# A three-stage kernel on one Trainium2 core: the last two chunks' second layers by eight plain products, added up in the PSUM banks, with totals and shares scaled ahead

## The chip, the cores and the metric

The kernel runs on one core of a Trainium2 chip. The metric is the device time of one execution in microseconds (us). Engine names as in the profile: PE is TensorE's matmuls, PEld its weight loads, DVE is VectorE, ACT is ScalarE, POOL is GpSimd, SP is SyncE, which here only issues transfers.

## The reference, cut to what matters

```python
x  = retention(q, k, v)                    # (2304, 512)
g  = np.maximum(x @ w_in, 0.0) ** 2        # first block, d_ff 2048
x  = g @ w_out                             # (2304, 512)
p  = probs / (probs.sum(-1, keepdims=True) + 1e-9)
for e in range(4):                         # four experts, 1024 hidden each
    h    = np.maximum(x @ w1[e], 0.0)
    out += p[:, e:e+1] * (h @ w2[e])
```

Everything is fp32; each product of two fp32 matrices is done as three matmuls, high part by high part, high by low and low by high.

## The kernel before, in words

Tokens are cut into five groups: four of 512 and one of 256. The hidden dimension is cut into chunks of 256: 8 chunks for the first block (numbers 0 to 7) and 16 for the experts. The experts' chunks are gone through twice. Pass 1 (chunks 8 to 23) serves groups 0, 1 and 4, and keeps the split weights in DRAM (`keep`). Pass 2 (chunks 24 to 39) serves groups 2 and 3 together, fetches the kept weights (`fetch`), and is where the change lies. `NW` is 40, so `NW - 2` and `NW - 1` are chunks 38 and 39; `split_w2`, for chunks 22 and 23, makes the second-layer weights of both.

In pass 2 both layers are done by a seven-product scheme (Strassen and Winograd) over 2 by 2 blocks. The first layer of a chunk (`first_layer`) is seven products of six matmuls each: A11 and then A12 into bank b1, S2 into b6, S3 and then A22 into b7, S1 and then S4 into b5. ACT copies the half-done b1 into `u0` (L865), before A12 is added into that bank; DVE adds (`add`, L853) and does relu times the token's expert share in one instruction (`relu`, L856). The shares lie in `rows` (`prow[3]` is the last expert's). Each result becomes an operand (`operand`, which calls `split`): ACT casts the high part (L130), POOL subtracts for the low part (L131). POOL also makes the differences t1 to t4 that the second layer needs (`minus`, L859); their operands are put off into the following chunk by the list `later`.

The second layer of chunk c (`second_layer`) runs one chunk later, in seven steps between the products of chunk c + 1's first layer: R4, H12, R3, H11, R1, R2, H22. A step is two banks with three matmuls each. R3 goes into the banks that hold R4, and H11 into those that hold H12, so that R3 waits until DVE has added R4 alone into its total, and H11 likewise. DVE adds every step into the totals e1 to e4 (`gather`, L939, two instructions a step). So a chunk is 42 + 42 matmuls.

The last chunk's second layer (`outputs`) is eight products of six matmuls each without the scheme, each with a bank of its own (a "place"): the totals are settled first (e2 gets e1 on DVE at L1129; POOL makes e3 and e4 at L992); then each place is added to its total (L1010), multiplied by the token's scale `back` (L1014 on DVE, L1012 on POOL) and sent out (L1017). `back` comes from DRAM and is halved on ACT (L987). The last place is done in two halves of 256 columns.

Every engine takes its instructions in the order in which the code issues them; a wait holds up all that stand behind it on that engine. The PSUM pool gives the 8 banks out in turn.

Of the kernel before, what the change touches and what calls it, by code (L numbers as in the profile page):

```python
# [6 lines left out]
F32 = mybir.dt.float32  # L7
# [4 lines left out]
ALU = mybir.AluOpType  # L12
# [14 lines left out]
NW1, NW2 = 8, 16  # L27
# [6 lines left out]
def tile_kernel(ctx, tc, qkT, kvn, v4d, mask, kdec, wd, w, probs, probs2, out, outT):  # L34
# [138 lines left out]
    def split_w2(c):  # L173

        hi = wp.tile([128, 2 * W2C], F32R, name="w2hi")
        lo = wp.tile([128, 2 * W2C], F32R, name="w2lo")
        w2t[c] = hi, lo
        w2s[c] = [t[:, :W2C].rearrange("p (f n) -> p f n", f=FT) for t in (hi, lo)]
        blk = [slice(BC * i, BC * (i + 1)) for i in range(8)]
        if c < NW1:  # L180
            for i in range(4):
                r = wraw.pop((c, 4 + i))
                yield from from_f64(r, hi[:, blk[i]], lo[:, blk[i]])
                load_piece()
# [361 lines left out]
    with tc.manual_schedule():  # L546
# [259 lines left out]
                    nc.sync.dma_start(out=out[tt * 128 : (tt + 1) * 128, :], in_=acc)  # L806

        spare = []
        taken, ops, prow, sums, later, loads = [0], {}, [], [], [], []

        def operand(src):
            t = gp.tile([128, FT, GT], F32R, name="ghi" if taken[0] % 2 else "glo")
# [15 lines left out]
        def first_layer(c):  # L828
# [33 lines left out]
            t3 = wrp.tile([128, GT], F32, name="wraw")  # L862
            b1 = bank()
            product(b1, A11, 7)
            nc.scalar.copy(out=u0, in_=b1)  # L865
# [29 lines left out]
            add(b11, b5, u1)  # L895
            relu(b11, b11, 1)
            o["11"] = operand(b11)

            def one():
                o["t1"] = operand(b12)  # L900
# [8 lines left out]
            def four():  # L909
                o["t4"] = operand(b21)  # L910

            if c < NW - 1:
                minus(b12, b12, b11)
                later.extend((one, two, three, four))
            yield
# [62 lines left out]
        def outputs(c):  # L978

            w2h, w2l = w2t[c]  # L980
            o = ops.pop(c)
            v = nc.vector
            back = []
            for i in range(2):
                t = wrp.tile([128, GT], F32, name="wraw")
                nc.sync.dma_start(out=t, in_=units_[i : i + 1, :].rearrange("o n -> (o n)").partition_broadcast(128))
                nc.scalar.activation(out=t, in_=t, func=ACTF.Copy, scale=0.5)  # L987
                back.append(t)
            e1, e2, e3, e4 = totals()
            for a, b in ((e3, e2), (e4, e3)):  # L990
                for d in range(2):
                    nc.gpsimd.tensor_tensor(out=a[d], in0=b[d], in1=a[d], op=ALU.subtract)  # L992
            for e, half, g, xs in (
                (e2, 0, 0, ("12", "22")), (e1, 0, 1, ("11", "21")), (e3, 1, 0, ("12", "22")), (e4, 1, 1, ("11", "21"))
            ):
                for d in range(2):
                    b = ps.tile([128, GT], F32, name="h", tag="ps")
                    n = 0
                    for f in range(2):
                        i = (H11, H12)[f] + half  # L1000
                        for a, y in ((w2h, 0), (w2h, 1), (w2l, 0)):
                            nc.tensor.matmul(
                                b, a[:, BC * i + 128 * d : BC * i + 128 * d + 128], o[xs[f]][:, y, :],
                                start=(n == 0), stop=(n == 5),
                            )
                            n += 1
                    r, m = 256 * half + 128 * d, GT // 2 if (half, g, d) == (1, 1, 1) else GT
                    for j in range(0, GT, m):
                        p = slice(j, j + m)
                        v.tensor_tensor(out=e[d][:, p], in0=e[d][:, p], in1=b[:, p], op=ALU.add)  # L1010
                        if (half, g, d) in ((0, 1, 0), (0, 1, 1), (1, 0, 0)):
                            nc.gpsimd.tensor_tensor(out=e[d], in0=e[d], in1=back[g], op=ALU.mult)  # L1012
                        else:
                            v.scalar_tensor_tensor(  # L1014
                                out=e[d][:, p], in0=e[d][:, p], scalar=1.0, in1=back[g][:, p], op0=ALU.mult, op1=ALU.mult
                            )
                        nc.sync.dma_start(out=outT[r : r + 128, GT * g + j : GT * g + j + m], in_=e[d][:, p])  # L1017

        def layer2(job):
            c, gs = job  # L1020
# [93 lines left out]
                s = scale(g, rest[:1])  # L1114
        sums += [yp.tile([128, 4, GT], F32, name=f"sums{i}", tag=f"acc{i}") for i in (2, 3)]
        for c in range(NW1 + NW2 + 1, NW):
            f, t = first_layer(c), second_layer(c - 1)
# [5 lines left out]
            if c == NW - 1:  # L1123
                for i in range(4):
                    next(t)
                    if i == 2:
                        e1, e2, _, _ = totals()
                        for d in range(2):
                            nc.vector.scalar_tensor_tensor(  # L1129
                                out=e2[d], in0=e1[d], scalar=1.0, in1=e2[d], op0=ALU.mult, op1=ALU.add  # L1130
                            )
# [3 lines left out]
        outputs(NW - 1)  # L1135


def _host(inputs):
# [75 lines left out]
```

## Time and profile before

| | us |
|---|---|
| time, median of 3 runs (lowest to highest) | 1205.81 (1205.4 to 1208.23) |
| time of the profiled execution | 1205.93 |
| its span, first to last instruction | 1204.1 |
| PE busy | 1188.4 (99% of the span) |
| DVE busy | 905.5 (75%) |
| POOL busy | 687.1 (57%) |
| ACT busy | 425.6 (35%) |

The profiled execution took 1.83 us more than its span. Start times in rows count from the first instruction. A matmul's row shows 0.39 us although one starts every 0.227 us, since they are pipelined; gaps between starts are the thing to read.

### The profile page before, as it was taken

How to read it: one execution, taken by the hardware profiler on the slowest of the kernel's cores; microseconds unless marked ns; L12 is line 12 of the kernel's file. 1: busy time of each engine (PE TensorE's matmuls, PEld its weight loads, DVE VectorE, ACT ScalarE, POOL GpSimd, SP SyncE). 2: the span in 40 equal slices, each digit the busy share in tenths (PEclk: the TensorE clock that was granted, in tenths of full speed). 3: DMA queues.
4: the chain of work that ended last, by engine and by line, in shares of the span. 5: the costliest groups of instructions: out<-in, count | busy, mean ns of one | idle time of the engine just before them, and what ended most of it. 6: DMA issues, size and time to landing. Idle time of an engine off the chain costs nothing.

```text
span 1204.1 us, 18090 instructions
## 1 busy us (share of the span) xinstructions
PE 1188.4 (99%) x6448; PEld 1001.1 (83%) x6448; DVE 905.5 (75%) x1543; ACT 425.6 (35%) x976; POOL 687.1 (57%) x686
## 2 busy tenths in 40 slices
PE   7999999999999999999999999999999999999997
PEld 7888888888888888888888888888888888888886
DVE  5877677787787689477877778777867787878778
ACT  3445433333333346534234334333412222222221
POOL 4656545455555426566444544644327777777777
PEclk9999999999999999999999999999999999999999
DMA  9921111111111100645355435555497546464551
GB/s 331 313 88 53 44 45 53 45 45 44 44 53 45 36 1 19 236 167 227 139 211 202 158 121 194 206 215 209 154 320 277 200 168 237 143 233 156 211 175 70
DMA packets 66513, 177.18 MB, mean 147 GB/s; under 512 B 9204, under 2 KB 17652, under 8 KB 66424
## 3 DMA queue, kind: packets, MB, share of 16 engines
q1 hardware_dynamic: 66136, 175.82, 41.0%
q8 instruction: 51, 0.84, 0.3%
q14 instruction: 38, 0.31, 0.1%
q10 hardware_dynamic: 288, 0.21, 0.1%
HBM read 113.33 MB, written 62.68 MB: 146 GB/s over the span
## 4 chain that ended last, share of the span: by engine, by line
PE 93%; DVE 4%; POOL 1%; ACT 1%; issue 1%; DMA 0%; SPq 0%; DVEq 0%; ACTq 0%
PE h L597 20%; PE o L793 17%; PE o L762 16%; PE h L631 13%; PE h L846 12%; PE h L929 11%; PE xo L438 1%; PE xo L450 1%; DVE pt L399 1%; PE qk L385 1%; DVE xl L721 1%; PE state L416 0%; DMA kv_n<-kvn 0%; DVE xl L473 0%; DVE sums L1010 0%
## 5 line engine op out<-in xcount | busy, mean ns | idle before, releaser
L131 POOL TENSOR_TENSOR glo<-r,ghi 128x512 fp32r<-128x512 f32 (+1 forms) x78 | 95.1, 1219 | 150.7 <-ACT ghi L130 136.6
L597 PE MATMUL h<-xl,w1hi 128*128 128x512 f32 (+1 forms) x448 | 154.0, 344 | 0.0
L597 PE MATMUL h<-xh,w1hi 128*128 128x512 f32 (+1 forms) x448 | 154.0, 344 | 0.0
L597 PE MATMUL h<-xh,w1lo 128*128 128x512 f32 (+1 forms) x448 | 153.9, 344 | 0.0
L801 DVE SCALAR_TENSOR_TENSOR oacc<-o,pr,oacc 128x512 f32<-128x512 f32 x150 | 109.6, 744 | 27.6 <-PE o L793 27.3
L939 DVE TENSOR_TENSOR sums<-sums,h 128x512 f32<-128x512 f32 x202 | 128.3, 677 | 1.2 <-PE h L929 1.2
L793 PE MATMUL o<-w2hi,ghi 128*128 128x512 f32 x320 | 124.8, 390 | 0.1
L793 PE MATMUL o<-w2hi,glo 128*128 128x512 f32 x320 | 124.7, 390 | 0.0
L793 PE MATMUL o<-w2lo,ghi 128*128 128x512 f32 x320 | 124.5, 389 | 0.0
L762 PE MATMUL o<-glo,w2hi 128*128 128x512 f32 (+1 forms) x320 | 117.8, 368 | 0.0
L762 PE MATMUL o<-ghi,w2hi 128*128 128x512 f32 (+1 forms) x320 | 117.7, 368 | 0.0
L762 PE MATMUL o<-ghi,w2lo 128*128 128x512 f32 (+1 forms) x320 | 117.7, 368 | 0.0
L605 DVE TENSOR_TENSOR r<-r 128x512 f32<-128x512 f32 (+1 forms) x72 | 58.0, 806 | 58.1 <-ACT r L601 57.9
L597 PEld LDWEIGHTS h<-xh,w1hi 128*128 128x128 f32 x448 | 84.8, 189 | 10.8
L597 PEld LDWEIGHTS h<-xl,w1hi 128*128 128x128 f32 x448 | 84.9, 189 | 10.6
L597 PEld LDWEIGHTS h<-xh,w1lo 128*128 128x128 f32 x448 | 84.8, 189 | 10.0
L770 DVE TENSOR_TENSOR y<-o,y 128x512 f32<-128x512 f32 (+1 forms) x140 | 86.1, 627 | 3.5 <-PE o L762 3.4
L846 PE MATMUL h<-xh,w1hi 128*128 128x512 f32 x224 | 88.1, 394 | 0.2 <-ACT r L865 0.2
L631 PE MATMUL h<-xh,w1lo 128*128 128x512 f32 x224 | 87.3, 390 | 0.0
L846 PE MATMUL h<-xh,w1lo 128*128 128x512 f32 x224 | 87.3, 390 | 0.0
L631 PE MATMUL h<-xh,w1hi 128*128 128x512 f32 x224 | 87.2, 389 | 0.0
L846 PE MATMUL h<-xl,w1hi 128*128 128x512 f32 x224 | 87.2, 389 | 0.0
(167 smaller groups left out, 2867.4 us busy)
## 6 DMA issues: line engine op xcount, KB each, us to landing
wraw<-wd SPq DMA_DIRECT2D x64, 256.0 KB, 2.7
wraw<-w SPq DMA_DIRECT2D x64, 256.0 KB, 2.9
kept<-w2hi SPq DMA_DIRECT2D x15, 768.0 KB, 4.3
kept<-w2lo SPq DMA_DIRECT2D x15, 768.0 KB, 6.0
w2hi<-kept SPq DMA_DIRECT2D x14, 768.0 KB, 5.1
w2lo<-kept SPq DMA_DIRECT2D x14, 768.0 KB, 6.7
qkt<-qkT SPq DMA_DIRECT2D x16, 576.0 KB, 6.1
kv_n<-kvn SPq DMA_DIRECT2D x16, 512.0 KB, 5.6
```

Of the source, the lines that this page charges most:

```text
L131: engine.tensor_tensor(out=lo, in0=src, in1=f32(hi), op=ALU.subtract)
L385: nc.tensor.matmul(qk[:, j, w : w + m], k_t[p, o : o + C], q_t[p, o : o + m], start=True, stop=True, skip_group_check=True,)
L597: nc.tensor.matmul(h, wk(a, f, k), group(x, g, k), start=(n == 0), stop=(n == 3 * KT - 1))
L605: nc.vector.tensor_tensor(out=r, in0=r, in1=r, op=ALU.mult)
L631: nc.tensor.matmul(o, a[:, i, k, :], slot(x, j)[:, k, :], start=(first and n == 0), stop=(n == 5), skip_group_check=True,)
L762: nc.tensor.matmul(o, a[:, f, 128 * m : 128 * m + 128], x[:, f, :], start=(n == 0), stop=(n == 3 * FT - 1))
L770: nc.vector.tensor_tensor(out=y, in0=o, in1=y, op=ALU.add)
L793: nc.tensor.matmul(o, a[:, f, 128 * m : 128 * m + 128], x[:, f, :], start=(n == 0), stop=(n == 3 * FT - 1))
L801: nc.vector.scalar_tensor_tensor(out=acc, in0=o, scalar=pr[:, tt, e : e + 1], in1=acc, op0=ALU.mult, op1=ALU.add)
L846: nc.tensor.matmul(o, a[:, i, k, :], slot(x, j)[:, k, :], start=(first and n == 0), stop=(n == 5), skip_group_check=True,)
L929: nc.tensor.matmul(b, a[:, BC * i + 128 * d : BC * i + 128 * d + 128], o[x][:, y, :], start=(first and n == 0), stop=(n == 2), skip_group_ ...
L939: v.tensor_tensor(out=e, in0=e, in1=b, op=op)
```

## The change

Chunks 38 and 39 no longer make t1 to t4 and t3. Both second layers are done by eight plain products (`plain_second`): chunk 38's go into eight banks (four new ones, and the four of chunk 39's first layer as they come free), and chunk 39's are added on top in the same banks, so that DVE adds one result to each total instead of gathering chunk 38's seven steps. The totals are settled and multiplied by `back` during chunk 39's first layer (`settle`), and the last expert's shares are multiplied by `back` before chunk 38 (`scale_shares`), so that its and chunk 39's results come out scaled already. `back` is loaded at the start of chunk 37 (`load_back`). For chunk 22 the four derived weight blocks are not made, kept or fetched.

```diff
-        whole = c < NW1 + NW2 - 1
+        whole = c < NW1 + NW2 - 2
...
-        return ((0, 1), (2, 8)) if c % NW2 != NW1 - 1 else ((0, 4),)
+        return ((0, 1), (2, 8)) if c % NW2 not in (NW1 - 2, NW1 - 1) else ((0, 4),)
...
-            if c == NW - 1:
+            if c >= NW - 2:
                 o["12"] = operand(b12)
...
-            if c < NW - 1:
+            if c < NW - 2:
                 minus(t3, b22, b12)
                 o["t3"] = operand(t3)
...
+        def plain_second():
+            e1, e2, e3, e4 = totals()
+            banks = [ps.tile([128, GT], F32, name="h", tag="ps") for _ in range(4)]
...
+            for c in (NW - 2, NW - 1):
+                w2h, w2l = w2t[c]
+                o = ops[c]
+                for k, (e, half, g, d) in enumerate(places):
+                    b = banks[k] if k < 4 else ops[NW - 1]["banks"][k - 4]
...
+                                start=(c == NW - 2 and n == 0), stop=(n == 5), skip_group_check=True,
...
+                    if c == NW - 2:
+                        yield
+                        continue
...
+                        nc.vector.tensor_tensor(out=e[:, p], in0=e[:, p], in1=b[:, p], op=ALU.add)
+                        nc.sync.dma_start(out=outT[r : r + 128, GT * g + j : GT * g + j + m], in_=e[:, p])
...
+        def scale_shares():
+            for i, t in enumerate(back):
                 nc.scalar.activation(out=t, in_=t, func=ACTF.Copy, scale=0.5)
+                x = prow[3][:, i, :]
+                scaled_by(nc.vector, x, t)
...
+        def settle():
+            v, g = nc.vector, nc.gpsimd
+            e1, e2, e3, e4 = totals()
+            for d in range(2):
+                v.scalar_tensor_tensor(out=e2[d], in0=e1[d], scalar=1.0, in1=e2[d], op0=ALU.mult, op1=ALU.add)
+            yield
+            for d in range(2):
+                g.tensor_tensor(out=e3[d], in0=e2[d], in1=e3[d], op=ALU.subtract)
+                scaled_by(v, e1[d], back[1])
+                yield
+            for d in range(2):
+                g.tensor_tensor(out=e4[d], in0=e3[d], in1=e4[d], op=ALU.subtract)
+                scaled_by(v, e2[d], back[0])
+                yield
...
         for c in range(NW1 + NW2 + 1, NW):
+            if c == NW - 3:
+                load_back()
+            if c == NW - 2:
+                scale_shares()
+            if c == NW - 1:
+                f, t, k = first_layer(c), None, settle()
+            else:
+                f, t = first_layer(c), second_layer(c - 1)
             for i, _ in enumerate(f):
-                if later and (c, i) != (NW - 2, 6):
+                if later:
                     later.pop(0)()
-                if c < NW - 1 or i % 2:
+                if c < NW - 1:
                     next(t)
+                    continue
+                next(k)
+                if i == 1:
+                    t = plain_second()
+                if i % 2:
+                    next(t)
...
+        for _ in (*k, *t):
+            pass
```

Where the instructions move, at the two places that matter. First ACT at the end of chunk 37 and the start of chunk 38. `wraw` in a cast is t3, the cast from `spare_xh_9063` behind the copies of chunk 37's other results is t1, and L865 is the copy `u0` of chunk 38. Before:

```order
L130 CAST ghi<-wraw 128x512
L130 CAST glo<-spare_xl_9064 128x512
L130 CAST ghi<-spare_xh_9063 128x512
L865 COPY r<-h 128x512
L130 CAST glo<-spare_xl_9064 128x512
```

And now (the same buffers have other numbers; `wraw` in L1018 is `back`):

```order
L130 CAST ghi<-wraw 128x512
L130 CAST glo<-spare_xl_9050 128x512
L130 CAST ghi<-spare_xh_9049 128x512
L1018 ACTIVATE wraw<-wraw 128x512 x2
L865 COPY r<-h 128x512
L130 CAST glo<-spare_xl_9050 128x512
```

The two halvings of `back` stand between t1's cast and the copy `u0` of chunk 38. Second, DVE at the same place: the relu of chunk 37's last block, chunk 36's last gather (H22) into e4, chunk 37's first (R4) into e2, and the first add of chunk 38. Before:

```order
L853 TENSOR_TENSOR spare_xl_9064<-h,r 128x512
L856 SCALAR_TENSOR_TENSOR spare_xl_9064<-spare_xl_9064,rows_8995 128x512
L939 TENSOR_TENSOR sums_9169<-sums_9169,h 128x512 x2
L939 TENSOR_TENSOR sums_9168<-sums_9168,h 128x512 x2
L853 TENSOR_TENSOR r<-h,r 128x512
L939 TENSOR_TENSOR sums_9168<-sums_9168,h 128x512 x2
```

And now:

```order
L853 TENSOR_TENSOR spare_xl_9050<-h,r 128x512
L856 SCALAR_TENSOR_TENSOR spare_xl_9050<-spare_xl_9050,rows_8981 128x512
L940 TENSOR_TENSOR sums_9155<-sums_9155,h 128x512 x2
L1024 SCALAR_TENSOR_TENSOR rows_8981<-rows_8981,wraw 128x512 x2
L940 TENSOR_TENSOR sums_9154<-sums_9154,h 128x512 x2
L853 TENSOR_TENSOR r<-h,r 128x512
L940 TENSOR_TENSOR sums_9154<-sums_9154,h 128x512 x2
```

The two multiplications of the shares stand between the gather of H22 and that of R4. Third, DVE at the end of the program, from the place before the last on. Before:

```order
L1010 TENSOR_TENSOR sums_9169<-sums_9169,h 128x512
L1014 SCALAR_TENSOR_TENSOR sums_9169<-sums_9169,wraw 128x512
L1010 TENSOR_TENSOR sums_9169<-sums_9169,h 128x256
L1014 SCALAR_TENSOR_TENSOR sums_9169<-sums_9169,wraw 128x256
L1010 TENSOR_TENSOR sums_9169<-sums_9169,h 128x256
L1014 SCALAR_TENSOR_TENSOR sums_9169<-sums_9169,wraw 128x256
```

And now, the last multiplications and all the additions:

```order
L1024 SCALAR_TENSOR_TENSOR sums_9155<-sums_9155,wraw 128x512 x2
L1005 TENSOR_TENSOR sums_9154<-sums_9154,h 128x512 x4
L1005 TENSOR_TENSOR sums_9155<-sums_9155,h 128x512 x3
L1005 TENSOR_TENSOR sums_9155<-sums_9155,h 128x256 x2
```

Nothing but additions is left behind the last products.

## Rows read from the trace of the kernel before

**Rows 1.** The page, part 1: busy time, share of the span, instructions.

```profile
PE 1188.4 (99%) x6448; PEld 1001.1 (83%) x6448; DVE 905.5 (75%) x1543; ACT 425.6 (35%) x976; POOL 687.1 (57%) x686
```

**Rows 2.** Waits of PEld over the run: total us, times, longest.

```profile
PEld h L846 <- ACT r L865: 3.0, 9, 0.6
```

**Rows 3.** Chain that ended last: start, us, what; its last long piece.

```profile
1195.42 1.79 DVE sums L1014
```

**Rows 4.** Timeline of PE around chunk 38's start: start us, duration us, instruction.

```profile
1147.33 0.39 PE L846 MATMUL h<-xh,w1hi 128*128 128x512 f32 x1
...
1153.90 0.39 PE L846 MATMUL h<-xh,w1lo 128*128 128x512 f32 x1
1154.13 0.62 PE L929 MATMUL h<-ghi,w2hi 128*128 128x512 f32 x2
...
1155.26 0.39 PE L929 MATMUL h<-ghi,w2lo 128*128 128x512 f32 x1
1155.54 0.50 PE L846 MATMUL h<-xh,w1hi 128*128 128x512 f32 x1
```

**Rows 5.** Timeline of PE at the end of chunk 38's second layer.

```profile
1184.04 0.39 PE L929 MATMUL h<-ghi,w2lo 128*128 128x512 f32 x1
...
1185.82 0.40 PE L1002 MATMUL h<-glo,w2hi 128*128 128x512 f32 x1
```

**Rows 6.** Timeline of PE, last matmul of the program.

```profile
1196.49 0.39 PE L1002 MATMUL h<-glo,w2lo 128*128 128x512 f32 x1
```

**Rows 7.** Timeline of DVE in the last stretch.

```profile
1185.93 2.41 DVE L1129 SCALAR_TENSOR_TENSOR sums<-sums 128x512 f32<-128x512 f32 x2
...
1199.59 0.41 DVE L1010 TENSOR_TENSOR sums<-sums,h 128x256 f32<-128x256 f32 x1
1200.04 0.42 DVE L1014 SCALAR_TENSOR_TENSOR sums<-sums,wraw 128x256 f32<-128x256 f32 x1
```

**Rows 8.** Timeline of ACT, chunk 38's start and the halving of `back`.

```profile
1154.38 0.62 ACT L130 CAST ghi<-spare_xh 128x512 fp32r<-128x512 f32 x1 [3.38 <-POOL spare_xh L859]
1154.91 0.58 ACT L865 COPY r<-h 128x512 f32<-128x512 f32 x1
...
1183.06 1.15 ACT L987 ACTIVATE wraw<-wraw 128x512 f32<-128x512 f32 x2
```

**Rows 9.** Timeline of DVE around chunk 38's start.

```profile
1148.60 2.47 DVE L939 TENSOR_TENSOR sums<-sums,h 128x512 f32<-128x512 f32 x4
1155.52 0.69 DVE L853 TENSOR_TENSOR r<-h,r 128x512 f32<-128x512 f32 x1 [4.46 <-ACT r L865]
```

**Rows 10.** Timeline of POOL around chunk 38's start.

```profile
1155.08 1.29 POOL L131 TENSOR_TENSOR ghi<-spare_xh,ghi 128x512 fp32r<-128x512 f32 x1 [0.73 <-ACT ghi L130]
1156.33 1.30 POOL L859 TENSOR_TENSOR spare_xl<-spare_xl,spare_xh 128x512 f32<-128x512 f32 x1
```

**Rows 11.** Timeline of DVE, one relu with two SBUF inputs, in chunk 38.

```profile
1167.10 0.82 DVE L856 SCALAR_TENSOR_TENSOR spare_xl<-spare_xl,rows 128x512 f32<-128x512 f32 x1
```

**Rows 12.** Timeline of POOL beside that relu.

```profile
1166.08 1.29 POOL L131 TENSOR_TENSOR ghi<-spare_xl,ghi 128x512 fp32r<-128x512 f32 x1 [1.36 <-ACT ghi L130]
1167.33 1.75 POOL L859 TENSOR_TENSOR wraw<-spare_xl,spare_xh 128x512 f32<-128x512 f32 x1
```

**Rows 13.** Groups by line and form, DVE, 1040 to 1166 us: count, busy us, mean ns.

```profile
L856 DVE SCALAR_TENSOR_TENSOR spare_xh<-spare_xh,rows 128x512 f32<-128x512 f32 x7 | 4.8, 692 | 0.2
```

**Rows 14.** Timeline of SP, last fetch issued at the end of chunk 36.

```profile
1131.70 0.47 SPq L232 DMA_DIRECT2D w1lo<-kept  x1
```

**Rows 15.** Transfers by kind: count, KB each, median us from issue to landing.

```profile
wraw<-units SPq DMA_DIRECT2D x2, 256.0 KB, 6.2
```

**Rows 16.** Stretches: busy us of PE, PEld, DVE, ACT, POOL; then the granted clock, DMA.

```profile
1196.88:1201.50 4.62, 0.00 (x0) 0.00 (x0) 3.41 (x7) 0.00 (x0) 1.45 (x1) 1.00 0.68 249
1201.50:1202.00 0.50, 0.00 (x0) 0.00 (x0) 0.00 (x0) 0.00 (x0) 0.00 (x0) 0.70 1.00 336
1202.00:1204.10 2.10, 0.00 (x0) 0.00 (x0) 0.00 (x0) 0.00 (x0) 0.00 (x0) 0.50 0.03 8
```

More of the change, by code (lines that the diff above doesn't have):

```diff
@@ L808, in tile_kernel @@
         spare = []
-        taken, ops, prow, sums, later, loads = [0], {}, [], [], [], []
+        taken, ops, prow, sums, later, loads, back = [0], {}, [], [], [], [], []
         def operand(src):
@@ L861, in first_layer @@
             u0, u1 = (tp.tile([128, GT], F32, name="r") for _ in range(2))
-            t3 = wrp.tile([128, GT], F32, name="wraw")
+            t3 = wrp.tile([128, GT], F32, name="wraw") if c < NW - 2 else None
             b1 = bank()
@@ L897, in first_layer @@
             o["11"] = operand(b11)
+            o["banks"] = b1, b6, b7, b5
             def one():
@@ L910, in four @@
                 o["t4"] = operand(b21)
-            if c < NW - 1:
+            if c < NW - 2:
                 minus(b12, b12, b11)
@@ L976, in totals, with load_back @@
             return ([t[:, 2 * i + d, :] for d in range(2)] for t in sums for i in range(2))
[L978 to L983, printed above, removed]
+        def plain_second():
+            e1, e2, e3, e4 = totals()
+            banks = [ps.tile([128, GT], F32, name="h", tag="ps") for _ in range(4)]
+            places = [(e[d], half, g, d) for e, half, g in ((e2, 0, 0), (e1, 0, 1), (e3, 1, 0), (e4, 1, 1)) for d in range(2)]
+            for c in (NW - 2, NW - 1):
[3 more added lines that the diff above has]
+                    b = banks[k] if k < 4 else ops[NW - 1]["banks"][k - 4]
+                    n = 0
+                    for f in range(2):
+                        i = (H11, H12)[f] + half
+                        x = o[("12", "22")[f] if g == 0 else ("11", "21")[f]]
+                        for a, y in ((w2h, 0), (w2h, 1), (w2l, 0)):
+                            nc.tensor.matmul(
+                                b, a[:, BC * i + 128 * d : BC * i + 128 * d + 128], x[:, y, :],
+                                start=(c == NW - 2 and n == 0), stop=(n == 5), skip_group_check=True,
+                            )
+                            n += 1
+                    if c == NW - 2:
+                        yield
+                        continue
+                    r, m = 256 * half + 128 * d, GT // 2 if (half, g, d) == (1, 1, 1) else GT
+                    for j in range(0, GT, m):
+                        p = slice(j, j + m)
+                        nc.vector.tensor_tensor(out=e[:, p], in0=e[:, p], in1=b[:, p], op=ALU.add)
+                        nc.sync.dma_start(out=outT[r : r + 128, GT * g + j : GT * g + j + m], in_=e[:, p])
+        def load_back():
             for i in range(2):
@@ L986, in outputs @@
                 nc.sync.dma_start(out=t, in_=units_[i : i + 1, :].rearrange("o n -> (o n)").partition_broadcast(128))
+                back.append(t)
+        def scale_shares():
+            for i, t in enumerate(back):
                 nc.scalar.activation(out=t, in_=t, func=ACTF.Copy, scale=0.5)
-                back.append(t)
-            e1, e2, e3, e4 = totals()
-            for a, b in ((e3, e2), (e4, e3)):
-                for d in range(2):
-                    nc.gpsimd.tensor_tensor(out=a[d], in0=b[d], in1=a[d], op=ALU.subtract)
@@ L993, in outputs @@
[L993 to L1017, printed above, removed]
@@ new lines, in scale_shares, with scaled_by @@
+                x = prow[3][:, i, :]
+                scaled_by(nc.vector, x, t)
+        def scaled_by(engine, x, t):
+            if engine is nc.vector:
+                engine.scalar_tensor_tensor(out=x, in0=x, scalar=1.0, in1=t, op0=ALU.mult, op1=ALU.mult)
+            else:
+                engine.tensor_tensor(out=x, in0=x, in1=t, op=ALU.mult)
+        def settle():
+            v, g = nc.vector, nc.gpsimd
+            e1, e2, e3, e4 = totals()
+            for d in range(2):
[9 more added lines that the diff above has]
+                yield
+            yield
+            yield
+            for d in range(2):
+                scaled_by(v, e3[d], back[0])
+                scaled_by(g, e4[d], back[1])
+            yield
@@ L1116, in tile_kernel @@
         for c in range(NW1 + NW2 + 1, NW):
-            f, t = first_layer(c), second_layer(c - 1)
+            if c == NW - 3:
[4 more added lines that the diff above has]
+                f, t, k = first_layer(c), None, settle()
+            else:
+                f, t = first_layer(c), second_layer(c - 1)
             for i, _ in enumerate(f):
-                if later and (c, i) != (NW - 2, 6):
+                if later:
                     later.pop(0)()
-                if c < NW - 1 or i % 2:
+                if c < NW - 1:
                     next(t)
-            if c == NW - 1:
-                for i in range(4):
-                    next(t)
[L1126 to L1131, printed above, removed]
+                    continue
[3 more added lines that the diff above has]
+                if i % 2:
+                    next(t)
             queue_weights((split_w1, c + 2), (split_w2, c + 1))
@@ L1134, in tile_kernel @@
                 loads.pop(0)()
-        outputs(NW - 1)
+        for _ in (*k, *t):
+            pass
 def _host(inputs):
```

## The prediction

> **What bounds the kernel now.** I read the page's busy times first: PE is busy for 99% of the span and no other engine for more than 75% [rows 1]. So a gain has to come from fewer matmuls, from PE's own waits or from what lies behind its last matmul, and a loss comes from anything that makes PE wait. The waits of PE's weight loads show how near the edge it runs: nine times it waited for the copy `u0` on ACT, 3.0 us in all [rows 2]. That wait is in pass 2, at product A12: the copy stands on ACT behind t1's cast, which waits for POOL [rows 8]. The reader is to see there that ACT idled for 3.38 us until POOL's difference was made, and that DVE in turn idled for 4.46 us until the copy was made [rows 9]. So in pass 2 ACT's queue is the late one, DVE has spare time only in front of that copy, and PE is just in time. Last, the chain that ended last leaves PE and runs through DVE's multiplications in the tail [rows 3]: DVE ends there at 1200.46 (1200.04 and 0.42) [rows 7], while the last matmul ends at 1196.88 (1196.49 and 0.39) [rows 6]. The tail behind PE is 3.58 us of DVE and then 3.64 us up to the span's end at 1204.1.
>
> **Matmuls.** Chunk 38's second layer goes from 42 matmuls to 48. From 1147.33 to 1154.13 thirty matmuls start [rows 4], so one costs 0.227 us, and six cost **+1.36 us**. At the end of chunk 38's old second layer seven slots took 1.78 us (1184.04 to 1185.82) [rows 5] where 1.59 would do. That wait belongs to t4, which is no longer made: **-0.19 us**.
>
> **The tail.** After the last matmul two half additions of 0.41 us are left [rows 7] instead of the 3.58 us of additions, multiplications and backlog: 3.58 - 0.82 = **-2.76 us**. The last send and what follows it I leave at 3.64 us. The nine sends leave in the same number and order, spaced by a place of six matmuls, so nothing should be queued in front of the last; if the present bunching costs it something, up to 0.5 us more is gained.
>
> **The new wait.** This is the term that decides. The two halvings of `back` stand on ACT between t1's cast and `u0`, and the two multiplications of the shares on DVE between the gathers of H22 and of R4. Neither is late for its data: `back` is sent for behind the fetch issued at 1131.70 [rows 14] and lands some 6.2 us after its issue [rows 15], 16 us ahead of its use. But ACT reaches the halvings only at 1154.91, behind t1's cast [rows 8]. DVE has gathered H22 by about 1149.8, the middle of the four gathers from 1148.60 [rows 9], and would now idle from there until the first halving is done, with the gather of R4 queued behind. R3 adds into R4's banks, so PE has to wait for that gather; it started R3 at 1154.13 [rows 4].
>
> Step by step: a halving is 0.575 us (1.15 for two) [rows 8], so the first ends at 1155.49, the second at 1156.06 and `u0` at 1156.64. DVE's first multiplication starts at 1155.52. At that time POOL works on t1's low part until 1156.37 and has the next difference queued behind [rows 10]. What that does is seen in a relu of the same kind (two SBUF inputs): it started at 1167.10, POOL's operation beside it ended at 1167.37 (1166.08 and 1.29) [rows 12], and the relu ended 0.55 us after that, at 1167.92 [rows 11]. POOL's next one then took 1.75 us instead of 1.29 and ended 1.16 us after the relu [rows 12]. They take turns. So the first multiplication ends at 1156.37 + 0.55 = 1156.92, POOL's difference at 1158.08, the second multiplication at 1158.63, and the first gather of R4 at 1159.25 (2.47 for four is 0.62 each) [rows 9]. R3 starts 5.12 us late. The old wait at A12 is swallowed: a start 0.28 us after the one before and a duration of 0.50 instead of 0.39 [rows 4], together 0.16 us. Net **+4.96 us**.
>
> The bounds: where the multiplications run without taking turns they take 0.69 us each [rows 13]; the gather is then done at 1157.52 and the net is 3.23 us. From above, the pair at the settling took 2.41 us [rows 7], less than my 3.11 from 1155.52 to 1158.63, so the turns are already the dear end. I take them, because POOL's two operations are in place at that very time [rows 10].
>
> The Trainium skill, "SBUF — State Buffer", section "Who interferes with whom", says that a VectorE instruction with two SBUF inputs contends with a GpSimd instruction that reads SBUF, and that the later one is blocked until the other is finished. The rows agree (0.82 us and 1.75 us); by that rule the whole sum below is +3.4, by the free rows +1.6.
>
> **What costs nothing, and its cover.** H11 needs the gather of H12: behind R4's second gather (1159.87), the add (0.69) and one gather it is there at 1161.2, and PE comes to it 12 matmuls after R3, at 1162.0. In chunk 39 DVE gets four adds (0.69), four relus (0.82) and eight multiplications, at 1.2 us each by the pair [rows 7], 15.7 us in all. Until the first added place is ready PE has 60 + 30 + 6 matmuls to do, 21.8 us; if the cover went, each us over would be lost whole. Chunk 38's 14 gathers and chunk 22's derived weights are dropped from engines for which PE doesn't wait there; I give that 0.3 us either way.
>
> **The sum.** 1.36 - 0.19 - 2.76 + 4.96 = +3.4 us. Against the profiled execution's 1205.93 (0.12 above the median of the runs) that is **1209.3 us**.
>
> **Rivals.** (1) *The clock falls in the new gap.* After the last matmul the granted clock stayed at 1.00, averaged 0.70 in the half us after 1201.50 and was 0.50 afterwards [rows 16]: it fell at about 1201.7, 4.8 us after PE stopped. The gap that I forecast reaches from 1154.29 (the end of the matmul that starts at 1153.90 [rows 4]) to 1159.25, 4.96 us. That is the same length within the error. At 1.2 instead of 2.4 GHz a matmul's slot grows by at most 0.227 us. No row shows how soon the clock comes back. If it takes as long as the fall, 4.8 us at half speed cost 2.4 us; at the other end nothing. 1.5 us more gives **1210.8**. The Trainium skill, "TensorE: Matmul & The Clock Gate", Part 1, says that an idle array is throttled to half its clock and gets it back after sustained work; the trace agrees with the first half, and no run here shows the second.
>
> (2) *The multiplications don't take turns with POOL.* Then the net wait is 3.23 us, the sum +1.6, the time **1207.6**. The relu of 0.69 us speaks for it [rows 13], the relu that waited against [rows 11, 12].
>
> (3) *No new wait, and the end is earlier: not slower.* This needs the first gather of R4 to be done by 1154.13, so the multiplications to start by about 1152.1, when `back` has long landed. Then the sum is 1.36 - 0.19 - 2.76 = -1.6, the time **1204.3**. It would be so if ACT did the halvings ahead of t1's cast. Against it: ACT idled for 3.38 us in front of that cast in this very place [rows 8], and the order puts the halvings behind.
>
> (4) *Chunk 39 is too full.* Multiplications of 1.79 us, as one was in the tail [rows 3], make DVE's work 20.4 of the 21.8 us, and POOL's subtractions are lengthened too. A backlog of 1 to 2 us would end at the last place: **1211**.
>
> **How the numbers follow.** Chances: the forecast 0.45, the clock 0.26, no turns 0.13, no wait 0.08, chunk 39 too full 0.06, something else that is faster 0.02. About 0.3% (3.6 us, so 1209.43 and 1202.19) is what a measurement of this kernel can tell from no change. The forecast, with 0.5 us either way, lies just under that bound: 0.20 of its 0.45 go above it. So slower is 0.20 + 0.26 + 0.06 = 0.52, faster 0.02, the rest, 0.46, within. The range is 1206.6 (no turns, with the sends' and pass 1's 0.8 us on top) to 1212.0 (clock at its dear end, with 0.3 more); it leaves out the case without a wait and the ends of the others.
>
> **What would show it.** In the profile after: PE idle for about 5 us at its first matmuls of R3 in chunk 38, ended by DVE's gather; two DVE multiplications there that start at about the first halving's end and last about 1.4 and 1.7 us; no PE wait at A12 of that chunk; 96 matmuls of the plain kind; under 1 us from the last matmul's end to DVE's last addition. The granted clock of the 5 us behind the gap decides (1). If PE runs through R3 without a gap, the main step is wrong; if a gap stands in chunk 39 or before the added places, (4).

## The result, and the profile after

The changed kernel takes 1212.27 us (median of 6 runs, 1210.94 to 1214.73), the kernel before, measured beside it, 1205.61 us (6 runs, 1205.03 to 1208.23). The ratio is 1.0052, 95% interval 1.0039 to 1.0065: 6.7 us slower, beyond the 0.3% that can be told from no change. It is 3.0 us over the forecast of 1209.3 and 0.3 us over the upper end of the range.

The profiled execution took 1214.73 us, with a span of 1212.9, and is the slowest of the six. Of the 8.8 us between it and the profiled execution of before, 1.1 us is there before the first block's first matmul of L597 starts (75.61 against 74.47), in code that is the same in both. I leave that share out. The page after, part 1, answers to [rows 1]:

```profile
PE 1192.0 (98%) x6454; PEld 1004.0 (83%) x6454; DVE 899.3 (74%) x1527; ACT 422.8 (35%) x969; POOL 672.8 (55%) x674
```

Six matmuls more, less work on DVE, ACT and POOL (of the two chunks only 38 made t1 to t4 before; chunk 39 had none), and PE busy for one per cent less of the span. The waits of PE and of its weight loads (total us, times, longest) tell where, beside [rows 2]:

```profile
PE h L930 <- DVE sums L940: 5.0, 1, 5.0
...
PEld h L846 <- ACT r L865: 2.5, 8, 0.3
...
PE h L631 <- ACT r L644: 2.4, 1, 2.4
```

L930 is the second layer's matmul (L929 before). Two waits are new: 5.0 us for the gather, which was forecast, and 2.4 us in pass 1, which was not. The copy `u0` has one wait less: the longest of them, in chunk 38, is swallowed.

**The gap in chunk 38.** Timeline of PE, beside [rows 4]:

```profile
1157.50 0.39 PE L846 MATMUL h<-xh,w1lo 128*128 128x512 f32 x1
1162.90 1.19 PE L930 MATMUL h<-ghi,w2hi 128*128 128x512 f32 x2 [5.02 <-DVE sums L940]
...
1168.16 0.70 PE L930 MATMUL h<-glo,w2hi 128*128 128x512 f32 x2
```

R3 should have started one slot after 1157.50, at 1157.73, and started 5.17 us late. Timeline of DVE there, beside [rows 9]:

```profile
1152.21 1.27 DVE L940 TENSOR_TENSOR sums<-sums,h 128x512 f32<-128x512 f32 x2
1159.16 3.00 DVE L1024 SCALAR_TENSOR_TENSOR rows<-rows,wraw 128x512 f32<-128x512 f32 x2 [5.68 <-ACT wraw L1018]
1162.08 1.27 DVE L940 TENSOR_TENSOR sums<-sums,h 128x512 f32<-128x512 f32 x2
```

The first row is the gather of H22, the last that of R4. Between them DVE idles for 5.68 us until ACT has halved the first half of `back`. Timeline of ACT, beside [rows 8]:

```profile
1157.98 0.62 ACT L130 CAST ghi<-spare_xh 128x512 fp32r<-128x512 f32 x1 [3.37 <-POOL spare_xh L859]
1158.51 1.14 ACT L1018 ACTIVATE wraw<-wraw 128x512 f32<-128x512 f32 x2
1159.56 0.56 ACT L865 COPY r<-h 128x512 f32<-128x512 f32 x1
```

And of POOL, beside [rows 10]:

```profile
1158.68 1.27 POOL L131 TENSOR_TENSOR ghi<-spare_xh,ghi 128x512 fp32r<-128x512 f32 x1 [0.73 <-ACT ghi L130]
1159.90 1.71 POOL L859 TENSOR_TENSOR spare_xl<-spare_xl,spare_xh 128x512 f32<-128x512 f32 x1
```

Read backwards, the chain is this: PE waits for a gather, the gather for two multiplications, these for the halvings, the halvings for t1's cast in front of them, and that cast for POOL. ACT and DVE idle meanwhile.

**The clock.** Stretches: length, busy us of PE, PEld, DVE, ACT, POOL; then the granted clock, DMA share, GB/s:

```profile
1157.89:1161.50 3.61, 0.00 (x0) 0.00 (x0) 2.34 (x2) 2.14 (x4) 2.88 (x3) 1.00 0.82 334
1161.50:1162.00 0.50, 0.00 (x0) 0.00 (x0) 0.50 (x1) 0.35 (x1) 0.11 (x1) 0.50 0.00 0
...
1162.90:1168.00 5.10, 5.10 (x12) 4.04 (x13) 4.04 (x7) 0.62 (x1) 3.23 (x3) 0.50 0.02 3
1168.00:1168.50 0.50, 0.50 (x3) 0.36 (x3) 0.10 (x1) 0.00 (x0) 0.00 (x0) 0.70 0.00 0
1168.50:1180.00 11.50, 11.50 (x52) 9.54 (x51) 10.47 (x16) 3.08 (x5) 5.03 (x4) 1.00 0.10 33
```

The clock fell from 1.00 (2.4 GHz) to 0.50 (1.2 GHz) while PE stood still, and was back 5.4 us after the matmuls had gone on (0.70 in the half us from 1168.00 puts it at 1168.3). The twelve matmuls from 1162.90 to 1168.16 took 5.26 us; at 0.227 us each they take 2.72. The clock cost 2.54 us.

**The tail.** The last matmul on PE and DVE's last additions, beside [rows 6, 7]:

```profile
1208.83 0.39 PE L994 MATMUL h<-ghi,w2lo 128*128 128x512 f32 x1
```

```profile
1209.33 0.75 DVE L1005 TENSOR_TENSOR sums<-sums,h 128x256 f32<-128x256 f32 x2 [0.67 <-PE h L994]
```

DVE ends at 1210.08, 0.86 us after PE (1209.22), and waited for PE in front of these additions: nothing is behind on it. From there to the span's end it is 2.82 us, where it was 3.64.

**Pass 1.** The wait that was not forecast is in chunk 22's first layer, at L631. DVE, ACT and PE there:

```profile
838.21 0.42 DVE L167 TENSOR_TENSOR cv_m<-wraw 128x256 f32<-128x256 f32 x1 [5.79 <-DMA wraw<-w]
```

```profile
839.13 0.41 ACT L130 CAST w1hi<-cv_d 128x256 fp32r<-128x256 f32 x1 [6.75 <-DVE cv_d L167]
...
841.57 0.58 ACT L644 COPY r<-h 128x512 f32<-128x512 f32 x1
```

```profile
842.20 0.50 PE L631 MATMUL h<-xh,w1hi 128*128 128x512 f32 x1 [2.42 <-ACT r L644]
```

Before, at the same place, the copy stood ahead of those casts, and one difference stood ahead of DVE's first add of this layer (L638):

```profile
834.65 0.59 ACT L644 COPY r<-h 128x512 f32<-128x512 f32 x1 [1.89 <-PE h L631]
```

```profile
836.28 0.43 DVE L167 TENSOR_TENSOR cv_m<-wraw 128x256 f32<-128x256 f32 x1 [1.98 <-DMA wraw<-w]
836.62 0.68 DVE L638 TENSOR_TENSOR r<-h,r 128x512 f32<-128x512 f32 x1
```

The weights of coming chunks are split in small steps, which pass 1 slips between its own instructions, one at each `tick`. Chunk 22's derived blocks were such steps. With them gone, the steps behind them come at earlier ticks, ahead of other instructions of the pass: the differences for chunk 23's first layer (L167) now meet a load that has not landed, DVE waits for it, ACT's cast waits for DVE, and the copy that PE needs stands behind that cast and three more. Behind this wait the clock stayed:

```profile
842.20:846.00 3.80, 3.80 (x16) 2.94 (x17) 3.34 (x5) 1.23 (x2) 1.05 (x2) 1.00 0.65 238
```

### The profile page after: what moved, and what is told of

Same layout as the page of the kernel before. It is cut to its first block, busy times and chain, and to the rows that moved or that the text cites. A ratio compares the mean times of both kernels' runs of the same rounds, so it can differ in the third digit from the quotient of the medians.

```text
span 1212.9 us, 18049 instructions
## 1 busy us (share of the span) xinstructions
PE 1192.0 (98%) x6454; PEld 1004.0 (83%) x6454; DVE 899.3 (74%) x1527; ACT 422.8 (35%) x969; POOL 672.8 (55%) x674
## 4 chain that ended last, share of the span: by engine, by line
PE 92%; DVE 2%; POOL 1%; DMA 1%; ACT 1%; issue 1%; DVEq 0%; ACTq 0%
PE h L597 20%; PE o L762 16%; PE o L793 16%; PE h L846 12%; PE h L631 12%; PE h L930 11%; PE h L994 2%; PE xo L438 1%; DMA kv_n<-kvn 1%; PE xo L450 1%; DVE xl L721 1%; PE qk L385 1%; DMA wraw<-w 0%; DVE pt L399 0%; PE state L416 0%
## 5 line engine op out<-in xcount | busy, mean ns | idle before, releaser
L597 PE MATMUL h<-xl,w1hi 128*128 128x512 f32 (+1 forms) x448 | 154.0, 344 | 0.0
L597 PE MATMUL h<-xh,w1hi 128*128 128x512 f32 (+1 forms) x448 | 154.0, 344 | 0.0
L597 PE MATMUL h<-xh,w1lo 128*128 128x512 f32 (+1 forms) x448 | 153.9, 344 | 0.0
L940 DVE TENSOR_TENSOR sums<-sums,h 128x512 f32<-128x512 f32 x188 | 119.7, 678 | 1.3 <-PE h L930 1.2
L597 PEld LDWEIGHTS h<-xl,w1hi 128*128 128x128 f32 x448 | 84.8, 189 | 10.7
L597 PEld LDWEIGHTS h<-xh,w1hi 128*128 128x128 f32 x448 | 84.8, 189 | 10.7
L597 PEld LDWEIGHTS h<-xh,w1lo 128*128 128x128 f32 x448 | 84.8, 189 | 10.0
L631 PE MATMUL h<-xh,w1hi 128*128 128x512 f32 x224 | 87.4, 390 | 2.4 <-ACT r L644 2.4
L631 PE MATMUL h<-xh,w1lo 128*128 128x512 f32 x224 | 87.2, 389 | 0.0
```

The lines of the kernel that those rows point to most:

```text
L597: nc.tensor.matmul(h, wk(a, f, k), group(x, g, k), start=(n == 0), stop=(n == 3 * KT - 1))
L631: nc.tensor.matmul(o, a[:, i, k, :], slot(x, j)[:, k, :], start=(first and n == 0), stop=(n == 5), skip_group_check=True,)
L940: v.tensor_tensor(out=e, in0=e, in1=b, op=op)
```

## The experiments

Each time is a median, and each ratio is to the kernel before, timed on the same chip (1205.76 us in the first four, 1205.74 in the last three).

**First: pass 1 as before.** Empty steps take the places of the steps that chunk 22 lost, so that the later steps come at the same ticks as before; the rest is the changed kernel.

```diff
-            for _ in range((3 if piece[0] == H11 else 1) if whole else 0):
+            for _ in range((3 if piece[0] == H11 else 1) if c < NW1 + NW2 - 1 else 0):
                 yield
-                o, x, y, op = todo.pop(0)
-                v.tensor_tensor(out=o, in0=x, in1=y, op=op)
+                if whole:
+                    o, x, y, op = todo.pop(0)
+                    v.tensor_tensor(out=o, in0=x, in1=y, op=op)
...
+            if f is split_w2 and c == NW1 + NW2 - 2:
+                yield
```

> The changed kernel, with an empty step in pass 1 wherever chunk 22's left-out work used to take one, so that everything behind stands where it stood before; the work itself stays left out. Theory: the changed kernel's 1212.3 us contains a PE wait of 2.4 to 2.8 us in chunk 22's first layer, because chunk 23's weight differences moved in front of it and wait for a load. Then this run has no such wait and takes 1209.6 to 1210.0 us. Rival: that wait belongs to the profiled execution alone (it was 2.4 us over the median of the runs); then 1212.3 us, the same within 0.5 us.

Measured: 1210.12 us (1209.38 to 1211.58, 5 runs), ratio 1.0036, 1.0024 to 1.0048. No wait of L631 (L635 in this kernel) for that copy is left, and the gap in chunk 38 is the same 5.02 us. So 2.15 us of the loss came from pass 1, by the order of its steps and not by their work. The two intervals overlap, but the second and the fourth experiment, with 12 and 11 runs, differ by the same edit and by 2.25 us.

**Second: the shares scaled a chunk sooner.** `back` is sent for at chunk 35, halved on ACT in chunk 36, and the multiplications stand on DVE in chunk 37, in the idle time in front of the add `u1`, written to a tile that is no longer used; chunks 38 and 39 read that tile.

```diff
-            p = prow[(c - NW1) % NW2 // (NW2 // 4)]
+            p = prow[2 if c >= NW - 2 else (c - NW1) % NW2 // (NW2 // 4)]
...
-            if c == NW - 3:
+            if c == NW - 5:
                 load_back()
-            if c == NW - 2:
-                scale_shares()
...
+                    if (c, i) == (NW - 4, 0):
+                        halve()
+                    if (c, i) == (NW - 3, 0):
+                        scale_shares()
```

> The changed kernel, with back loaded two chunks sooner into the place of expert 0's shares, halved during chunk 36, and the scaled shares written in chunk 37 into the place of expert 2's shares, on DVE between R4's gathers and the add that waits for ACT's copy. Theory: the gap of 5.0 us in front of R3 in chunk 38 and the half clock behind it (12 matmuls in 5.26 us instead of 2.72, so 2.5 us) are both gone: 1212.3 - 5.0 - 2.5 = 1204.8 us. Rival 1: the clock does not hang on that gap; then 1207.3 us. Rival 2: the loss lies elsewhere (chunk 39 too full, six matmuls); then 1211 to 1212.3 us.

Measured: 1206.52 us (1204.56 to 1209.49, 12 runs), ratio 1.0007, 0.9998 to 1.0017. The gap is gone and the clock stays at 1.00 from 1130 to 1180. So 5.75 us of the loss hung on that one place. The 1.7 us over the expectation has a row on PE, at A12 of chunk 37:

```profile
1140.77 0.50 PE L846 MATMUL h<-xh,w1hi 128*128 128x512 f32 x1 [0.79 <-ACT r L865]
```

With the longer first matmul that is 0.9 us. For the rest, 0.8, the trace has a candidate. This kernel keeps the wait of pass 1, and in its profiled execution (1207.93 us) the clock fell behind it:

```profile
840.83 0.79 PE L631 MATMUL h<-xh,w1hi 128*128 128x512 f32 x1 [2.46 <-ACT r L644]
```

```profile
841.00:844.00 3.00, 3.00 (x8) 2.35 (x9) 1.88 (x3) 0.21 (x1) 0.85 (x2) 0.50 0.57 187
```

Eight matmuls, from 840.83 to 844.35, took 3.52 us instead of 1.82, so the wait cost 1.7 us more here than in the changed kernel's profiled execution, where the clock stayed at 1.00 behind nearly the same wait (2.42 us). The runs fit two such prices: the five whose mean granted clock is 1.000 have a median of 1205.86 us, the seven at 0.998 or 0.999 one of 1207.93. The traces show it for one execution of each kernel only.

**Third: only one multiplication in front of R4's gather**, the other behind it; the rest is the changed kernel.

```diff
-                x = prow[3][:, i, :]
-                scaled_by(nc.vector, x, t)
+            share(0)
...
+                    if (c, i) == (NW - 2, 0):
+                        share(1)
```

> The changed kernel, with only the first of the two multiplications of the shares in front of R4's gather in chunk 38, the second behind it. Theory: the gap in front of R3 shrinks by the second multiplication, 1.5 to 1.7 us, to about 3.4 us, which is less than the 3.6 us after which the granted clock fell within the gap of the changed kernel and the 4.8 us at the end of the kernel before; the clock stays at 1.00, and the time falls by 1.6 + 2.5 to 1208.2 us. Rival: the fall of the clock is not the gap's, or its length does not matter; then 1210.7 us.

Measured: 1212.35 us (1209.8 to 1212.88, 5 runs), ratio 1.0047, 1.0035 to 1.0059: a miss. The gap shrank as it should, but the clock fell nonetheless. PE, and the stretches from there on:

```profile
1161.97 0.70 PE L930 MATMUL h<-ghi,w2hi 128*128 128x512 f32 x2 [3.35 <-DVE sums L940]
```

```profile
1158.62:1161.97 3.35, 0.00 (x2) 0.03 (x1) 2.07 (x3) 2.14 (x4) 2.62 (x3) 1.00 0.86 351
1161.97:1163.00 1.03, 1.03 (x5) 0.86 (x6) 1.03 (x3) 0.61 (x1) 0.39 (x1) 1.00 0.10 32
1163.00:1164.00 1.00, 1.00 (x5) 0.79 (x4) 1.00 (x3) 0.01 (x1) 0.91 (x1) 0.69 0.00 0
1164.00:1166.00 2.00, 2.00 (x6) 1.56 (x5) 2.00 (x5) 0.34 (x1) 1.62 (x2) 0.50 0.00 0
1166.00:1167.00 1.00, 1.00 (x4) 0.82 (x3) 1.00 (x3) 0.28 (x1) 0.65 (x1) 0.60 0.00 0
```

R3 and the next matmuls run at 1.00, and the fall comes 1.4 us after they have gone on, about 1163.4 (0.69 in the stretch from 1163.00); half speed lasts to about 1166.8 (0.60 in that from 1166.00). By rows the gap is 1.67 us shorter and half speed costs some 1.7 us (half of 3.4) instead of 2.54, together 2.5 us less than in the changed kernel. The profiled execution has these 2.5 us: from R3's slot to DVE's last addition it took 49.79 us (1158.46 to 1208.25), the changed kernel's 52.35 (1157.73 to 1210.08). The medians don't show them (5 runs, 3 us apart). Part of the answer is in pass 1, which is the same in both kernels. PE there, and two stretches:

```profile
841.52 0.50 PE L631 MATMUL h<-xh,w1hi 128*128 128x512 f32 x1 [1.81 <-ACT r L644]
```

```profile
842.00:843.00 1.00, 1.00 (x6) 0.75 (x4) 0.88 (x2) 0.00 (x0) 0.56 (x1) 0.76 0.12 27
843.00:845.50 2.50, 2.50 (x7) 1.94 (x6) 1.38 (x2) 1.12 (x2) 0.00 (x0) 0.50 0.95 342
```

After a wait of only 1.81 us the clock fell at about 842.5 (0.76 in the us from 842.00), and nine matmuls, from 842.32 to 845.96, took 3.64 us instead of 2.04: 1.6 us that the changed kernel's profiled execution did not pay. The fastest run, 1209.8 us, is what the rows give without that cost, and its mean granted clock is 0.998 where the other four have 0.997. Whether those four all paid it, no trace shows; so far the miss of the median stays open.

**Fourth: the first and the second together.** No edit beyond theirs.

> Both of the first two edits together. Theory: the two losses are independent and both go: 1204.8 - 2.5 = 1202.3 us, below the 1205.6 us of the kernel before by what the prediction gave to the tail and the matmuls (1.36 - 0.19 - 2.76 = -1.6 us) and 0.8 us more in the last send, so 1202.3 to 1204.0 us. Rival: the wait in pass 1 was one execution's; then the same as the second run, 1204.8 us.

Measured: 1204.27 us (1203.05 to 1205.7, 11 runs), ratio 0.9986, 0.9977 to 0.9994: ahead of both kernels, and 0.3 us over the expected span. The two repairs add up: the sooner shares are worth 5.85 us on the first experiment's kernel and 5.75 on the changed one. DVE, POOL and PE in chunk 37 show what is left:

```profile
1131.60 3.11 DVE L1027 SCALAR_TENSOR_TENSOR rows<-rows,rows 128x512 f32<-128x512 f32 x2
```

```profile
1132.42 1.74 POOL L131 TENSOR_TENSOR ghi<-spare_xl,ghi 128x512 fp32r<-128x512 f32 x1
1134.12 1.74 POOL L863 TENSOR_TENSOR spare_xh<-spare_xh,spare_xl 128x512 f32<-128x512 f32 x1
```

```profile
1137.05 0.50 PE L850 MATMUL h<-xh,w1hi 128*128 128x512 f32 x1 [0.78 <-ACT r L869]
```

DVE's time in that place is free, but POOL's is not: its two operations take 1.74 us instead of 1.29 [rows 10], t1's cast and the copy `u0` behind it come 0.9 us later, and PE waits at A12.

**Fifth: the kernel before with the wait alone.** Nothing of the change but the early load and halvings, which move here from the last stage, and the two multiplications at the start of chunk 38, whose product nothing reads.

```diff
+            if c == NW - 3:
+                load_back()
+            if c == NW - 2:
+                wait_only()
...
+        def wait_only():
+            for i, t in enumerate(back):
+                nc.scalar.activation(out=t, in_=t, func=ACTF.Copy, scale=0.5)
+                nc.vector.scalar_tensor_tensor(
+                    out=prow[2][:, i, :], in0=prow[3][:, i, :], scalar=1.0, in1=t, op0=ALU.mult, op1=ALU.mult
+                )
```

> The kernel before with one addition: the scales are sent for at the start of chunk 37 (into the shares of the first expert, which are no longer read), halved on ACT at the start of chunk 38 and multiplied with the last expert's shares on DVE in front of the gather of R4, as in the changed kernel, but the product is written to a place that nothing reads; the halving in the last stage falls away. Nothing else of the change is in it. If the wait at R3 and what hangs on it explain the loss of pass 2, it costs about 5.0 us of gap and about 2.5 us at the lower clock: 1205.8 + 7.5 = 1213.3 (1212.3 to 1214.0). Rival: the gap needs the lighter chunk 38 of the change or is made up later; then the time is within 1 us of the kernel before, 1205.8. If the gap comes but the clock holds, 1210.8.

Measured: 1212.72 us (1211.82 to 1214.0, 5 runs), ratio 1.0054, 1.0041 to 1.0066: 7.0 us dearer than the kernel before, within the expected span. PE and DVE in chunk 38:

```profile
1159.34 1.19 PE L929 MATMUL h<-ghi,w2hi 128*128 128x512 f32 x2 [5.02 <-DVE sums L939]
```

```profile
1155.60 3.00 DVE L991 SCALAR_TENSOR_TENSOR rows<-rows,rows 128x512 f32<-128x512 f32 x2 [5.69 <-ACT rows L990]
```

The same gap, the same turns, and the clock at 0.50 from about 1157.2 to 1164.0. Four instructions at the wrong place in two queues are enough for a loss of this size, without the rest of the change.

**Sixth: the multiplications behind R4's gather**, on the first experiment's kernel.

```diff
-                x = prow[3][:, i, :]
-                scaled_by(nc.vector, x, t)
...
+                    if (c, i) == (NW - 2, 0):
+                        share(0)
+                        share(1)
```

> The first experiment's kernel with one thing moved: on DVE the two multiplications of the shares stand behind the gather of R4 instead of in front of it; the loading and the halvings stay where they are. If the gap is only a matter of the order in DVE's queue, R3 finds R4 gathered and the 5.0 us and the 2.5 us of the clock go; what is left is the copy u0, which the halvings make 1.15 us later, so PE should wait about 1.2 us at A12: 1210.1 - 7.5 + 1.2 = 1203.8 (1203.2 to 1204.8), clock 1.00 throughout. Rival: the same DVE work only moves the wait to the next thing behind it (the add u1 and the gather of H12, on which H11 waits); then 2 to 3 us come back there: 1206 to 1207.

Measured: 1206.3 us (1204.95 to 1207.37, 11 runs), ratio 1.0003, 0.9994 to 1.0012: the rival was right. PE, DVE, and a stretch:

```profile
1156.08 0.50 PE L850 MATMUL h<-xh,w1hi 128*128 128x512 f32 x1 [0.95 <-ACT r L869]
...
1159.36 0.73 PE L934 MATMUL h<-glo,w2hi 128*128 128x512 f32 x2 [1.63 <-DVE sums L944]
```

```profile
1155.07 3.04 DVE L1030 SCALAR_TENSOR_TENSOR rows<-rows,wraw 128x512 f32<-128x512 f32 x2 [4.51 <-ACT wraw L1022]
```

```profile
1150.00:1180.00 30.00, 27.43 (x120) 22.07 (x119) 24.69 (x34) 7.49 (x13) 20.95 (x16) 1.00 0.33 116
```

R3 has no wait now. A12 waits for `u0`, which stands behind the halvings, and H11 for the gather of H12, which stands behind the multiplications: 2.6 us in two parts instead of 5.0 in one. The clock stays at 1.00 over both. A late producer costs something in either place; moved behind one consumer it holds up the next.

**Seventh: each multiplication where POOL is idle too**, on the fourth experiment's kernel, with loading and halving one chunk sooner.

```diff
-            if c == NW - 5:
+            if c == NW - 6:
                 load_back()
...
+                    if i == 5 and c in (NW - 4, NW - 3):
+                        scale_shares(c - (NW - 4))
                     next(t)
-                    if (c, i) == (NW - 4, 0):
+                    if (c, i) == (NW - 5, 0):
                         halve()
-                    if (c, i) == (NW - 3, 0):
-                        scale_shares()
```

> The fourth experiment's kernel, with the scales sent for and halved one chunk sooner, and the two multiplications of the shares apart: each stands on DVE right behind the relu of the third result, one in chunk 36 and one in chunk 37, where GpSimd is idle for 1.4 us in front of its next subtraction. If the 0.3 us that the fourth experiment was over its expectation came from the turns that the two multiplications took with GpSimd, the wait at A12 of chunk 37 goes and the time is 0.8 to 1.2 us shorter: 1203.3 (1202.8 to 1203.8). Rival: each multiplication makes the relu behind it meet a GpSimd operation instead, and the wait only moves: 1204.3.

Measured: 1202.88 us (1201.35 to 1204.03, 8 runs), ratio 0.9976, 0.9965 to 0.9986: the fastest of all, 2.9 us ahead of the kernel before. DVE, and POOL beside the first multiplication:

```profile
1124.96 0.68 DVE L1026 SCALAR_TENSOR_TENSOR rows<-rows,rows 128x512 f32<-128x512 f32 x1
...
1143.77 0.68 DVE L1026 SCALAR_TENSOR_TENSOR rows<-rows,rows 128x512 f32<-128x512 f32 x1
```

```profile
1125.85 1.29 POOL L131 TENSOR_TENSOR ghi<-spare_xl,ghi 128x512 fp32r<-128x512 f32 x1 [1.35 <-ACT ghi L130]
```

The same instruction takes 0.68 us here and 1.5 there (3.00 and 3.11 for two): it ends before POOL's next one begins. The rival was half right. The relu behind now meets a POOL operation that is already running:

```profile
1127.10 1.30 POOL L863 TENSOR_TENSOR wraw<-spare_xl,spare_xh 128x512 f32<-128x512 f32 x1
```

```profile
1127.47 1.47 DVE L860 SCALAR_TENSOR_TENSOR spare_xl<-spare_xl,rows 128x512 f32<-128x512 f32 x1
```

In the kernel before, DVE came first and POOL paid (0.82 and 1.75 us [rows 11, 12]); here POOL comes first and DVE pays, and DVE's time is free in that place. In the list of waits none of PE's matmuls of pass 2 is left; its weight loads have seven, 2.1 us in all.

## Why the prediction was right, and where it fell short

The direction and the main step were right; the size was short, by the clock and by pass 1. The terms, forecast and read from the profile after:

| term | forecast, us | measured, us |
|---|---|---|
| six more matmuls, t4's wait | +1.17 | +1.19 (R3 to the last matmul) |
| tail behind the last matmul | -2.76 | -2.72 (0.86 instead of 3.58) |
| last send and what follows | 0 (up to -0.5) | -0.82 (2.82 instead of 3.64) |
| wait at R3, net | +4.96 | +5.01 (5.17 late, less 0.16) |
| clock in the gap | rival, +1.5 (0 to 2.4) | +2.54 |
| pass 1 | 0.3 either way | +2.42 (2.15 by the first experiment) |
| sum | +3.4 | +7.6 |

The first row is 45.93 us from 1162.90 to 1208.83, less 42.36 from 1154.13 [rows 4] to 1196.49 [rows 6], less the clock's 2.54, plus the old wait's 0.16. The 0.19 us that the prediction gives to t4 the profile puts down to ACT's halving of `back` (L987); the step in which PE waited is gone either way. The medians differ by 6.7; the 0.9 us between that and the rows' sum is within the runs' spread. The range's lower end, 1206.6, is 0.2 below its own terms (1207.6 less 0.8); nothing hangs on it.

**The new wait** came out step by step. Shifted by the 3.60 us by which R3's slot is later (1157.73 against 1154.13 [rows 4]), the forecast had the first multiplication at 1159.12, the second's end at 1162.23 and R3 at 1162.85; the rows have 1159.16, 1162.16 and 1162.90. The fifth experiment shows that this wait alone, put into the kernel before, makes a loss of the same size. The multiplications took turns with POOL, so rival (2) was wrong; the seventh experiment shows the same instructions at 0.68 us where POOL was idle. The Trainium skill, "SBUF — State Buffer", section "Who interferes with whom", says that the later of the two is blocked until the other is finished. The rows agree: 3.00 us for two where POOL worked, and 1.71 us for POOL's operation between them.

**The clock**, rival (1), was the step that was not taken into the forecast, though its length argument (4.96 us of gap, 4.8 us to the fall) said that it was even. It came, and at the dear end: 2.54 us. The argument was weak too: the clock fell 3.6 us into this gap, and in pass 1 it fell behind a gap of 1.81 us in the third experiment and not behind one of 2.42 us in the changed kernel, so the length of the gap alone does not decide it. The price of 1.5 was the middle between nothing and 2.4, for want of a row on the return. The return took 5.4 us after the matmuls had gone on. The Trainium skill, "TensorE: Matmul & The Clock Gate", Part 1, says that the full clock comes back only after sustained work; this is the half of the rule that no row of before showed, and the runs agree with it.

**Pass 1** is the step that failed: "dropped from engines for which PE doesn't wait there; I give that 0.3 us either way". The work was indeed off PE's path, but it also held places in a sequence of background steps. Removing it moved everything behind it forward in the queues of DVE and ACT. Four of the differences of L167 now come ahead of the first add of that layer on DVE (L638) where one did; the prediction read only the end of the program so closely. This term and the clock carried the time past the range's upper end, which held the clock's dear end but no pass 1 above 0.3.

**The rest.** Rival (3), no wait, was wrong as argued: ACT came to the halvings behind t1's cast. Rival (4) was wrong: PE has no wait in chunk 39, and the additions of the places wait for PE, not PE for them. The last send's 3.64 us shortened by 0.82, more than the 0.5 allowed. It is the new tail's doing: the other kernels with that tail have 2.85 to 2.87 us there, the fifth experiment's, with the old one, 3.65. The DMA engines were full behind the last send before (share 1.00 to 1.03 from 1200.0 to 1202.0) and are not now (0.44 to 0.81 from 1210.0 to 1211.5), and a send took up to 2.5 us to land where it now takes at most 2.0. So the bunching is some 0.5 of it; the other 0.3 stays open. H11 had no wait after the gap, as forecast; in the sixth experiment, where the multiplications stand in front of H12's gather and R3 doesn't wait, it has 1.63 us.

## What to carry to other kernels

A small instruction is priced by its place in its queue: ask what stands in front of it there and who waits behind it, and put it where its inputs are long done and its neighbours idle (with that and the steps of pass 1 put back, 6.7 us slower became 2.9 us faster with the same arithmetic). Work that is taken out of a paced sequence shifts all that follows it, so the order of instructions is to be read there as well as where work was added. A wait of some microseconds on PE is to be priced with the clock after it, and with two prices: behind nearly the same wait in pass 1 (2.42 and 2.46 us) the clock cost nothing in one profiled execution and 1.7 us in another.

## What the runs showed of the hardware that was not expected

- The clock fell after PE was at work again: in the third experiment PE stood for 3.35 us, went on at 1.00, and the fall came 1.4 us later. In the changed kernel and the fifth experiment it fell inside the gap, 3.6 and 2.9 us after the last matmul's end. Gaps of 0.95 and 1.63 us in the sixth experiment cost no clock, nor did the one of 2.42 us in the changed kernel's pass 1. One of 1.81 us in pass 1 (third experiment) did, 1.0 us after the matmuls had gone on, and so did one of 2.46 us (second experiment), just as they went on.
- Where the fall came inside the gap, the clock was back 5.4 us after the matmuls had gone on (changed kernel) and 4.7 us (fifth experiment); in the third experiment half speed lasted only 3.4 us, and as long in pass 1 of the second and the third.
- POOL's operation is lengthened too when the two take turns (1.29 to 1.74 us; DVE's from 0.68 to about 1.5), so an instruction in DVE's idle time can still cost PE a wait: 0.78 us in the fourth experiment. Which of the two pays changed with which started first (seventh experiment).
